# First two pairs loaded four tokens a row and turned in 112x128 blocks, second unit's values issued later

## The chip, the cores and the metric

The kernel runs on one core of one Trainium2 chip. The metric is the device time of one execution in microseconds (us); a median of several runs is given. The core has TensorE (matrix products, results in PSUM), VectorE, ScalarE, GpSimd, SyncE (SP, which here only issues transfers) and 16 DMA engines that all queues share.

## What is computed

Sigmoid attention, then a mixture of experts that sends each token to one expert:

```python
scores = q @ k^T / sqrt(64) - log(448)          # 8 batches, 12 heads, 448 tokens, 64 wide
attn   = sigmoid(scores)
x      = (attn @ v) as [8*448 tokens, 768]
logits = x @ w_gate                              # 8 experts
e      = argmax(logits); g = softmax(logits)[e]
out    = g * (relu(x @ w1[e]) @ w2[e])           # 768 -> 1024 -> 768
```

All arrays are 32-bit floats.

## The kernel before

Attention works on pairs of heads (48 pairs g, two heads of 64 on the 128 partitions) and on units of two pairs (24 units). A unit has seven steps (ST = KC = 7): a step takes every seventh token of k as 64 keys. For each step `scores(s)` multiplies k by q for both pairs (L562), ScalarE turns each pair's scores into weights by a sigmoid (`squash`, L549), and `weighted(s)` multiplies them with the values (L576) two steps behind the scores. TensorE executes in the order written; in the first steps that is scores of step s, then weighted sums of step s - 2.

k and q must stand with the head's 64 components on the partitions. From pair 2 on, `load_pair` brings them in pieces of 32 columns (128 bytes, eight DMAs a pair, q of pairs 3, 7, 9 and 11 through GpSimd's queue and the rest through SP's) and VectorE transposes 32x32 blocks (`turn`, L533). The first two pairs go another way, since nothing runs yet: `first_pair` loads each tile with one DMA, seven tokens a row (1792 bytes; k through SP, q through ScalarE's queue), and `first_turn` turns it on TensorE with 14 products by a slice of the identity (64x64, both heads beside each other; the trace records each as two), whose result VectorE (k) or ScalarE (q) copies from PSUM. Until the data are there TensorE runs 32 products of ones (`warm_up`, L540).

The values of a pair (`load_values`) come with seven tokens a row: pair 0 through ScalarE's queue, pairs 1 to 15 through GpSimd's; even pairs in one DMA, odd ones in two.

`attention` writes the order out by hand: `first_pair` for 0 and 1, the gate's weights, values of 0 and 1, warm-up, the turns, `load_pair` for 2 and 3, `load_values` for 2 and 3, then GpSimd's `blank_records` and `gate_columns`, then the steps. `READY` says behind which steps later pairs are loaded and transposed: the k of unit 2 (pairs 4, 5) is loaded from step 0 on, and so on. Tiles rotate: kn, qn, kt, qt and vn have four buffers, the weights of the sigmoid eight, the scores four PSUM banks. From step 36 on the expert layer's matmuls (L222, L241) are mixed with attention, and they fill the rest of the time.

Of the kernel before, what the change touches and what calls it, by code (L numbers as in the profile page):

```python
# [10 lines left out]
F32 = mybir.dt.float32  # L11
# [8 lines left out]
P = 128  # L20
# [5 lines left out]
def tile_sigmoid_attention_top1_moe(  # L26
# [18 lines left out]
    nc = tc.nc  # L45
    B, H, S, D = q.shape
# [3 lines left out]
    NP = H // 2  # L50
# [16 lines left out]
    small = ctx.enter_context(tc.tile_pool(name="small", bufs=1))  # L67
    ps_moe = ctx.enter_context(tc.tile_pool(name="ps_moe", bufs=2, space=bass.MemoryType.PSUM))

    ident = const.tile([P, P], F32, name="ident")  # L70
# [39 lines left out]
    def gate_columns():  # L110
        nc.gpsimd.tensor_copy(wgp[:, :, 0:E], wg)

    def blank_records():

        blank = hpool.tile([P, 1024], U32, tag=f"hl{KF - 2}", name="blank")
        blank3 = blank[:, : E * NT // P * 2].rearrange("p (r w) -> p r w", w=2)
        for w, val in enumerate((int(BIG), 0)):
            nc.gpsimd.iota(blank3[:, :, w], pattern=[[0, E * NT // P]], base=val, channel_multiplier=0)
        return lambda: nc.sync.dma_start(recs.rearrange("(p r) w -> p r w", p=P), blank3)
# [339 lines left out]
    DK = P // 2  # L459
    KC = S // DK  # L460
    ops = {}
    NG = B * NP
    OWN = [slice(h * D, (h + 1) * D) for h in range(2)]

    def quarter(g, h):

        return OWN[h if g % 2 == 0 else 1 - h]

    def load_pair(g):
        if g >= NG:  # L470
            return
        b, hp = divmod(g, NP)
        for nm, src in (("k", k), ("q", q)):
            t = apool.tile([P, S // 32, 32], F32, tag=nm + "n", bufs=4, name=f"{nm}n_{g}")
            eng = nc.gpsimd if nm == "q" and g in Q_POOL else nc.sync
            for h in range(2):
                for f in range(D // 32):
                    a = 2 * h + f
                    eng.dma_start(  # L479
                        t[32 * a : 32 * (a + 1)],  # L480
                        src[b, 2 * hp + h, :, 32 * f : 32 * (f + 1)].rearrange("(j r) s -> r j s", r=32),
                    )
            ops[g, nm + "n"] = t

    def both_heads(to, src, g, eng):
        b, hp = divmod(g, NP)
        eng.dma_start(to, src[b, 2 * hp : 2 * hp + 2].rearrange("h (p c) d -> (h p) (c d)", c=KC))

    def first_pair(g):

        t = wpool.tile([P, 1024], F32, tag="wst", bufs=RAWS_AHEAD, name=f"first_{g}")
        for n, (src, eng) in enumerate(((k, nc.sync), (q, nc.scalar))):
            both_heads(t[:, n * S : (n + 1) * S], src, g, eng)
        ops[g, "first"] = t

    def first_turn(g):

        t = ops.pop((g, "first"))
        for n, nm in enumerate("kq"):
            ps = score_tile(f"first_{g}_{nm}")  # L500
            for c in range(KC):
                for h in range(2):
                    rows, at = OWN[h], n * S + c * D
                    nc.tensor.matmul(
                        ps[rows, c * DK : (c + 1) * DK], t[rows, at : at + D], ident[rows, rows], start=True, stop=True
                    )
            to = apool.tile([P, S], F32, tag=nm + "t", bufs=4, name=f"{nm}t_{g}")
            if nm == "k":
                nc.vector.tensor_copy(to, ps[:, :S])
                ops[g, nm] = to.rearrange("d (c p) -> d c p", c=KC)  # L510
            else:
                nc.scalar.copy(to.rearrange("d (p c) -> d p c", c=KC), ps[:, :S].rearrange("d (c p) -> d p c", c=KC))
                ops[g, nm] = to

    def load_values(g):
        if g >= NG:
            return
        b, hp = divmod(g, NP)
        eng = nc.scalar if g == 0 else nc.gpsimd if g < V_POOL else nc.sync
        t = apool.tile([P, KC, D], F32, tag="vn", bufs=4, name=f"vn_{g}")  # L520
        if g % 2 == 0:
            both_heads(t.rearrange("p c d -> p (c d)"), v, g, eng)
        else:
            for h in range(2):
                eng.dma_start(t[quarter(g, h)], v[b, 2 * hp + h].rearrange("(p c) d -> p c d", c=KC))
        ops[g, "v"] = t
# [9 lines left out]
    def warm_up(n):  # L536

        ps = ps_moe.tile([P, 512], F32, tag="moe", name="ps_warm")
        for _ in range(n):
            nc.tensor.matmul(ps[:, :P], ones, ones, start=True, stop=True)  # L540

    ats, psv = {}, {}
# [9 lines left out]
    def score_tile(name):  # L552
        return ps_sc.tile([P, 512], F32, tag="sc", name=f"sc_{name}")

    def scores(s):
        u, c = divmod(s, ST)
        two = [2 * u + n for n in range(2)]
        pss = [score_tile(f"{g}_{c}") for g in two]
        for g, ps in zip(two, pss):
            for h in range(2):  # L560
                ks = ops[g, "k"][OWN[h], c]
                nc.tensor.matmul(ps[quarter(g, h), :S], ks, ops[g, "q"][OWN[h]], start=True, stop=True)  # L562
        for g, ps in zip(two, pss):
            squash(g, c, ps)
# [42 lines left out]
    def attention():  # L607

        order = ExitStack()
        order.enter_context(tc.manual_schedule())  # L610
        for g in range(2):
            first_pair(g)
        nc.gpsimd.dma_start(wg, w_gate.rearrange("(t p) e -> p t e", p=P))
        load_values(0)
        load_values(1)
        warm_up(WARM)
        first_turn(0)
        first_turn(1)
        for g in (2, 3):
            load_pair(g)  # L620
        for g in (2, 3):
            load_values(g)
        write_blank = blank_records()
        gate_columns()
        pend_gate = None
        done_av = 0

        def values(to):
            nonlocal done_av
            while done_av < min(to, N_ST):  # L630
                weighted(done_av)
                done_av += 1
                yield

        def steps(first, n, to):

            vs = values(to)
            for m in range(first, min(first + n, N_ST)):
                scores(m)
                next(vs, None)  # L640
            for _ in vs:
                pass

        for s in range(N_ST + 11):
            u, i = divmod(s, ST)
            if s in FIRST:
                wts.load(FIRST[s])
            if START - 3 < s < START:
                wts.ahead(s - START + 3, 2)
            if s < ALONE:  # L650
                steps(s, 1, s - 1)
            elif s == ALONE:
                steps(s, 1, s)
            elif i == ST - 1:
                steps(s - ST + 2, ST, s + 1)
            if s == START + 1:
                write_blank()
            elif s == START + 11:
                put_records(0)
            yield s, MIX[0]  # L660
            if s == PB + 3:
                gate_a(0)
            if i in READY and s < N_ST:
                READY[i](u)
            gb = s - PB
            if gb >= 0:
                b, r = divmod(gb, PB)
                r -= 3 if b == 0 else 2
                at = ("a" if b else None, "b", None, "c", "l", None) + (("d", "p", "e") if b else (None,) * 3 + ("d", "e"))
                what = at[r] if 0 <= r < len(at) else None  # L670
                if what == "a":
                    gate_a(b)
                elif what == "b":
                    pend_gate = gate_b(b)
                elif what == "c":
                    pend_gate = gate_c(b, *pend_gate)
                    gate_out[b] = pend_gate[0]
                elif what == "l":
                    load_regs(b)
                elif what == "d":  # L680
                    gate_d(b, *pend_gate)
                elif what == "p":
                    put_records(b)
                elif what == "e":
                    gate_e(b)
                if 3 <= r < 3 + KD // 2:
                    for t in range(2):
                        low_half(b, 2 * (r - 3) + t)
            yield s, MIX[1]
            if i in (1, 5):  # L690
                while turned:
                    token_rows(*turned.pop(0))
        order.close()
# [19 lines left out]
    for s, n in attention():  # L713
        if s >= START:
            more(n)
# [400 lines left out]
```

## Time and profile before

| | |
|---|---|
| median of 3 runs | 811.66 us (811.09 to 811.83) |
| profiled execution | 811.07 us, its span from first to last instruction 809.4 us |
| TensorE busy | 800.4 us, 99% |
| VectorE, ScalarE, GpSimd busy | 403.3, 398.1, 142.4 us |
| mean granted TensorE clock | 0.998 of full speed |
| DMA | 120.69 MB, mean 149 GB/s |

PE is TensorE and PEld its weight loads, DVE is VectorE, ACT ScalarE, POOL GpSimd; a q behind the name (SPq, POOLq) is the engine's sequencer, which issues transfers. L562 is line 562 of the kernel. Busy time of a pipelined TensorE is not TensorE at its peak. A DMA queue's share is the time that its packets took, over 16 engines' time in the window; q1 is SP's queue, q10 ScalarE's and q0 GpSimd's.

### The profile page before, as it was taken

To read this page: it belongs to the slowest core of one execution; us is meant where nothing else is said; L and a number is where in the kernel's file an instruction comes from. 1 tells how busy PE (TensorE), PEld (TensorE's weight loads), DVE (VectorE), ACT (ScalarE), POOL (GpSimd) and SP (SyncE) were. 2 spreads that over 40 slices of the span, in tenths; PEclk is the share of its full clock that TensorE was granted. 3 is DMA by queue.
4 is the path that set the end of the run, shared out by engine and by line. 5 is a ranking of instruction groups with operands and counts; after the bars stand their busy time and mean duration, and the time that the engine had idled before them with its cause. 6 is when DMAs were issued, how large, how long until landed. Compare 5 with 4: busy or idle time off the path is not lost.

```text
span 809.4 us, 15601 instructions
## 1 busy us (share of the span) xinstructions
PE 800.4 (99%) x5792; PEld 613.4 (76%) x5792; DVE 403.3 (50%) x870; ACT 398.1 (49%) x710; POOL 142.4 (18%) x212
## 2 busy tenths in 40 slices
PE   9999999999999999999999999999999999999996
PEld 5547678677687686786776876977867868999895
DVE  2466457344473265453562534833555325855561
ACT  5874745545635536446354455365463562233251
POOL 4442302110041000310022100320015001422101
PEclk9999999999999999999999999999999999999999
DMA  9999765495374663853748746548535422767761
GB/s 161 153 188 220 208 149 122 118 214 133 89 180 112 171 155 84 202 139 97 175 107 148 186 115 144 132 115 199 113 104 161 112 57 65 204 181 254 256 208 37
DMA packets 287123, 120.69 MB, mean 149 GB/s; under 512 B 200163, under 2 KB 279030, under 8 KB 287041
## 3 DMA queue, kind: packets, MB, share of 16 engines
q1 hardware_dynamic: 277792, 99.03, 51.8%
q0 software_dynamic: 8816, 19.91, 9.3%
q8 instruction: 47, 0.77, 0.4%
q10 hardware_dynamic: 432, 0.69, 0.2%
q14 instruction: 36, 0.29, 0.1%
HBM read 97.35 MB, written 23.07 MB: 149 GB/s over the span
## 4 chain that ended last, share of the span: by engine, by line
PE 95%; DMA 2%; SPq 1%; issue 1%; ACT 1%; DVE 1%; POOL 0%; POOLq 0%; DVEq 0%
PE ps L222 29%; PE ps L241 28%; PE sc L562 16%; PE av L576 15%; PE ps L926 2%; PE ps L906 2%; PE psg L275 1%; DMA kn<-in_k_dram 1%; SPq L479 1%; DMA wst<-in_moe_w_dram 0%; PE few L949 0%; ACT w1h L147 0%; PE pl L293 0%; DVE w2l L148 0%; PE pg L413 0%
## 5 line engine op out<-in xcount | busy, mean ns | idle before, releaser
L549 ACT ACTIVATE at<-sc,bias_s 128x448 f32<-128x448 f32 x336 | 196.2, 632 | 133.0 <-PE sc L562 132.0
L562 PE MATMUL sc<-qt,kt 64*64 64x448 f32 x1344 | 173.4, 544 | 0.3 <-DVE qt L533 0.3
L576 PE MATMUL av<-at,vn 64*64 64x448 f32 x1344 | 172.0, 537 | 0.0
L257 POOL DMA_DIRECT2D out_dram<-ob x96 | 61.6, 653 | 473.7 <-DVE ob L252 398.7
L241 PE MATMUL ps<-hh,w2l 128*128 128x448 f32 x384 | 142.3, 371 | 0.0
L241 PE MATMUL ps<-hh,w2h 128*128 128x448 f32 x384 | 141.8, 369 | 0.3 <-ACT w1h L147 0.3
L222 PE MATMUL ps<-xl,w1h 128*128 128x448 f32 x384 | 141.3, 368 | 0.0
L222 PE MATMUL ps<-xh,w1l 128*128 128x448 f32 x384 | 141.1, 367 | 0.0
L241 PE MATMUL ps<-hl,w2h 128*128 128x448 f32 x384 | 141.0, 367 | 0.0
L222 PE MATMUL ps<-xh,w1h 128*128 128x448 f32 x384 | 140.4, 366 | 0.0
L434 DVE STREAM_TRANSPOSE xt<-av 128x448 f32<-128x448 f32 x48 | 31.0, 646 | 211.4 <-ACT x L588 210.9
L562 PEld LDWEIGHTS sc<-qt,kt 64*64 64x64 f32 x1344 | 77.6, 189 | 61.5 <-issue 28.1
L576 PEld LDWEIGHTS av<-at,vn 64*64 64x64 f32 x1344 | 63.6, 132 | 59.8 <-issue 25.6
L227 ACT ACTIVATE hh<-ps 128x448 fp32r<-128x448 f32 x64 | 35.2, 550 | 146.1 <-PE ps L222 146.0
L147 ACT CAST w2h<-wst 128x512 fp32r<-128x512 f32 x96 | 62.0, 668 | 79.4 <-PE ps L241 67.1
L222 PEld LDWEIGHTS ps<-xl,w1h 128*128 128x128 f32 x384 | 72.1, 188 | 10.8 <-issue 5.2
L241 PEld LDWEIGHTS ps<-hh,w2h 128*128 128x128 f32 x384 | 72.2, 188 | 10.2 <-issue 4.2
L241 PEld LDWEIGHTS ps<-hh,w2l 128*128 128x128 f32 x384 | 72.2, 188 | 9.1 <-issue 3.6
L222 PEld LDWEIGHTS ps<-xh,w1l 128*128 128x128 f32 x384 | 72.1, 188 | 9.1 <-issue 3.5
L222 PEld LDWEIGHTS ps<-xh,w1h 128*128 128x128 f32 x384 | 72.1, 188 | 6.4 <-issue 0.7
L241 PEld LDWEIGHTS ps<-hl,w2h 128*128 128x128 f32 x384 | 72.2, 188 | 5.9 <-issue 0.4
L228 DVE SCALAR_TENSOR_TENSOR hl<-ps,hh 128x448 fp32r<-128x448 f32 x64 | 39.7, 621 | 71.1 <-ACT hh L227 69.4
(166 smaller groups left out, 756.3 us busy)
## 6 DMA issues: line engine op xcount, KB each, us to landing
wst<-in_moe_w_dram SPq DMA_DIRECT2D x48, 512.0 KB, 4.2
wst<-in_moe_w_dram SPq DMA_DIRECT2D x56, 384.0 KB, 4.0
x_tok<-xt SPq DMA_DIRECT2D x64, 168.0 KB, 4.5
out_dram<-ob POOLq DMA_DIRECT2D x96, 112.0 KB, 3.3
kn<-in_k_dram SPq DMA_DIRECT2D x184, 56.0 KB, 4.2
qn<-in_q_dram SPq DMA_DIRECT2D x168, 56.0 KB, 2.9
raw<-in_moe_w_dram SPq DMA_DIRECT2D x12, 512.0 KB, 4.7
kept<-in_moe_w_dram SPq DMA_DIRECT2D x12, 512.0 KB, 6.4
```

Of the source, the lines that this page charges most:

```text
L147: nc.scalar.copy(hi, st)
L222: nc.tensor.matmul(ps[:, :S], a[:, ws], b_, start=(t == 0 and n == 0), stop=(t == KD - 1 and n == 2))
L227: nc.scalar.activation(hh[:, :S], ps[:, :S], AF.Relu)
L228: nc.vector.scalar_tensor_tensor(hl[:, :S], ps[:, :S], 0.0, hh[:, :S].bitcast(F32), op0=ALU.max, op1=ALU.subtract)
L241: nc.tensor.matmul(ps[:, :S], a, b_, start=(j == 0 and n == 0), stop=(j == KF - 1 and n == 2))
L257: nc.gpsimd.dma_start(out[b * S : (b + 1) * S, cols].rearrange("(j r) f -> r j f", r=32), obv[32 * i : 32 * (i + 1)])
L434: nc.vector.transpose(xts[b, n][:, :, t, :], pv.rearrange("p (j s) -> p j s", s=32))
L549: nc.scalar.activation(at, ps[:, :S], AF.Sigmoid, bias=bias_s, scale=SCALE)
L562: nc.tensor.matmul(ps[quarter(g, h), :S], ks, ops[g, "q"][OWN[h]], start=True, stop=True)
L576: nc.tensor.matmul(psv[g][OWN[h], :S], ops[g, "v"][rows, c, :], at[rows], start=(c == 0), stop=(c == KC - 1))
L906: nc.tensor.matmul(pss[j], a[:, js], b_, start=(t == 0 and m == 0), stop=(t == KD - 1 and m == 2))
L926: nc.tensor.matmul(pss[h], a, b_[:, cs], start=(n == 0 and i == 0 and m == 0), stop=(n == 3 and i == 1 and m == 2),)
```

## The change

k and q of pairs 0 and 1 are loaded with four tokens a row on 112 partitions: one DMA a head, and the two heads side by side in each token's 128 columns, so that the pieces that land are 64 floats (256 bytes). A block of 112 tokens by 128 columns is then turned by one transposition, four for a tile, and the copy from PSUM puts the tokens in order (both copies with a strided read; k gets the view with every seventh token that all other pairs have). The values of pairs 2 and 3 are no longer issued before the steps but after the scores of the sixth step (s == 5), behind a copy of one element on GpSimd that reads that step's sigmoid weights of pair 0.

```diff
--- before.py
+++ after.py
@@ -486,31 +486,31 @@
         b, hp = divmod(g, NP)
         eng.dma_start(to, src[b, 2 * hp : 2 * hp + 2].rearrange("h (p c) d -> (h p) (c d)", c=KC))
 
+    FC = 4
+
     def first_pair(g):
 
+        b, hp = divmod(g, NP)
         t = wpool.tile([P, 1024], F32, tag="wst", bufs=RAWS_AHEAD, name=f"first_{g}")
         for n, (src, eng) in enumerate(((k, nc.sync), (q, nc.scalar))):
-            both_heads(t[:, n * S : (n + 1) * S], src, g, eng)
+            part = t[: S // FC, n * 512 : (n + 1) * 512].rearrange("p (c h d) -> p h c d", h=2, c=FC)
+            for h in range(2):
+                eng.dma_start(part[:, h], src[b, 2 * hp + h].rearrange("(p c) d -> p c d", c=FC))
         ops[g, "first"] = t
 
     def first_turn(g):
 
         t = ops.pop((g, "first"))
+        rows = S // FC
         for n, nm in enumerate("kq"):
             ps = score_tile(f"first_{g}_{nm}")
-            for c in range(KC):
-                for h in range(2):
-                    rows, at = OWN[h], n * S + c * D
-                    nc.tensor.matmul(
-                        ps[rows, c * DK : (c + 1) * DK], t[rows, at : at + D], ident[rows, rows], start=True, stop=True
-                    )
+            for c in range(FC):
+                part = t[:rows, n * 512 + c * P : n * 512 + (c + 1) * P]
+                nc.tensor.transpose(ps[:, c * rows : (c + 1) * rows], part, ident[:rows, :rows])
             to = apool.tile([P, S], F32, tag=nm + "t", bufs=4, name=f"{nm}t_{g}")
-            if nm == "k":
-                nc.vector.tensor_copy(to, ps[:, :S])
-                ops[g, nm] = to.rearrange("d (c p) -> d c p", c=KC)
-            else:
-                nc.scalar.copy(to.rearrange("d (p c) -> d p c", c=KC), ps[:, :S].rearrange("d (c p) -> d p c", c=KC))
-                ops[g, nm] = to
+            copy = nc.vector.tensor_copy if nm == "k" else nc.scalar.copy
+            copy(to.rearrange("d (p c) -> d p c", c=FC), ps[:, :S].rearrange("d (c p) -> d p c", c=FC))
+            ops[g, nm] = to.rearrange("d (p c) -> d c p", c=KC) if nm == "k" else to
 
     def load_values(g):
         if g >= NG:
@@ -618,8 +618,6 @@
         first_turn(1)
         for g in (2, 3):
             load_pair(g)
-        for g in (2, 3):
-            load_values(g)
         write_blank = blank_records()
         gate_columns()
         pend_gate = None
@@ -653,6 +651,11 @@
                 steps(s, 1, s)
             elif i == ST - 1:
                 steps(s - ST + 2, ST, s + 1)
+            if s == 5:
+                pace = small.tile([1, 1], F32, name="pace")
+                nc.gpsimd.tensor_copy(pace, ats[0, s][0:1, 0:1])
+                for g in (2, 3):
+                    load_values(g)
             if s == START + 1:
                 write_blank()
             elif s == START + 11:
```

## Rows read from the trace of the kernel before

**Rows 1.** The page: busy time of the engines; DMA queue of ScalarE (packets, MB, share).

```profile
PE 800.4 (99%) x5792; PEld 613.4 (76%) x5792; DVE 403.3 (50%) x870; ACT 398.1 (49%) x710; POOL 142.4 (18%) x212
...
q10 hardware_dynamic: 432, 0.69, 0.2%
```

**Rows 2.** The chain that ended last, 0 to 70 us: start, length, what.

```profile
7.41 2.12 SPq L479
...
11.63 5.36 DMA kn<-in_k_dram
...
18.33 0.60 PE sc L562
...
66.55 3.50 PE ps L222 x16
```

**Rows 3.** Timeline of ScalarE, 13 to 22 us: start, length, instructions, idle before.

```profile
15.16 1.35 ACT L549 ACTIVATE at<-sc,bias_s 128x448 f32<-128x448 f32 x2 [0.16 <-PE sc L562]
...
18.16 0.64 ACT L549 ACTIVATE at<-sc,bias_s 128x448 f32<-128x448 f32 x1 [0.16 <-PE sc L562]
...
20.27 1.33 ACT L549 ACTIVATE at<-sc,bias_s 128x448 f32<-128x448 f32 x2 [0.17 <-PE sc L562]
```

**Rows 4.** Timeline of VectorE, 16 to 29 us.

```profile
17.01 0.65 DVE L533 STREAM_TRANSPOSE kt<-kn 128x448 f32<-128x448 f32 x1 [1.51 <-DMA kn<-in_k_dram]
...
27.91 0.65 DVE L533 STREAM_TRANSPOSE qt<-qn 128x448 f32<-128x448 f32 x1 [2.56 <-DMA qn<-in_q_dram]
```

**Rows 5.** DMA queues, 2 to 6 us: packets, MB, share of 16 engines.

```profile
DMA packets 1674, 1.24 MB, mean 310 GB/s; under 512 B 1050, under 2 KB 1674, under 8 KB 1674
...
q10 hardware_dynamic: 427, 0.68, 49.2%
```

**Rows 6.** DMA queues, 11 to 14 us.

```profile
q0 software_dynamic: 153, 0.44, 72.1%
q1 hardware_dynamic: 1186, 0.15, 48.2%
```

**Rows 7.** DMA queues, 14 to 15 us.

```profile
q1 hardware_dynamic: 1085, 0.13, 128.0%
```

**Rows 8.** Timeline of TensorE, 3.8 to 8 us.

```profile
4.47 1.03 PE L504 MATMUL sc_first_k<-ident,first 64*64 64x64 f32 x28
...
7.78 0.55 PE L562 MATMUL sc<-qt,kt 64*64 64x448 f32 x2
```

**Rows 9.** Timeline of all engines, 743.05 to 743.7 us.

```profile
743.13 0.54 PEld L844 LDWEIGHTS px<-ident,xo 112*128 112x128 f32 x4
...
743.62 0.19 PEld L241 LDWEIGHTS ps<-hl,w2h 128*128 128x128 f32 x1
```

**Rows 10.** Timeline of VectorE, 0 to 24 us.

```profile
7.18 0.62 DVE L509 COPY kt<-sc_first_k 128x448 f32<-128x448 f32 x1 [1.01 <-PE sc_first_k L504]
```

**Rows 11.** Transfers of the first tiles: count, ns of one issue (min/median/max).

```profile
L487 SPq DMA_DIRECT2D first<-in_k_dram x2: 399/410/420, 0.9 to 1.3; - x2
```

**Rows 12.** DMA queues, 16 to 18 us.

```profile
q1 hardware_dynamic: 1016, 0.13, 41.5%
```

**Rows 13.** DMA queues, 670 to 680 us.

```profile
q1 hardware_dynamic: 1373, 0.51, 19.2%
```

**Rows 14.** Windows of two us: engines, then TensorE clock, DMA share, GB/s.

```profile
0.00:2.00 2.00, 0.70 (x7) 0.71 (x8) 0.37 (x3) 1.14 (x1) 1.31 (x12) 1.00 0.06 11
```

**Rows 15.** Timeline of GpSimd, 6 to 12 us.

```profile
7.15 0.58 POOL L487 DMA_DIRECT2D vn<-in_v_dram  x1
9.16 1.05 POOL L525 DMA_DIRECT2D vn<-in_v_dram  x2 [1.43 <-DMA wg<-in_moe_w_gate_dram]
...
10.78 0.24 POOL L111 COPY wgp<-wg 128x48 f32<-128x48 f32 x1
```

**Rows 16.** DMA issues, 7 to 7.5 us: count, KB, us to landing.

```profile
vn<-in_v_dram POOLq DMA_DIRECT2D x1, 224.0 KB, 8.3
```

**Rows 17.** DMA issues, 21.3 to 21.6 us.

```profile
vn<-in_v_dram POOLq DMA_DIRECT2D x1, 224.0 KB, 3.6
```

## The prediction

> **What bounds the kernel now.** I read the page first. TensorE is busy for 99% of the span [rows 1], so what can still move is where TensorE starts late or waits; the edit lies in the first 25 us, so only that stretch can answer. Next comes the chain that ended last, in order of time. Its front is not TensorE but the second unit's k: SP's queue, held for 2.12 us on one issue, then a kn transfer of 5.36 us, and only at 18.33 us the scores; from there to the expert matmuls at 66.55 us it is TensorE [rows 2]. The reader should see two things in it: TensorE's first scores set nothing, because the chain before 18.33 us is DMA; and what is won or lost at 18.33 us is handed down. How long TensorE stands there is read best from the sigmoids, which follow the scores at 1.50 us a step: the eighth step (first of unit 2) begins at 18.16, so the ninth should begin at 19.66 and begins at 20.27 [rows 3]. The stall is worth 0.61 us. It ends when k and q of pair 3 have been transposed, and the k transpose waited for its transfer until 17.01 [rows 4].
>
> What then bounds the transfers? The DMA windows answer: 2 to 6 us go at 310 GB/s with the big rows of the first pairs [rows 5]; from 11 to 14 us SP's queue, in 128-byte pieces, moves 1186 packets in 3 us while GpSimd's queue takes 72.1% of the engines [rows 6]; in the next microsecond, with GpSimd's done, it moves 1085 in one [rows 7]. The front is DMA-bound work of all three queues until kn of pair 3 has landed.
>
> **The change, part by part.**
>
> *Turning.* Now the four tiles are 112 recorded matmuls (28 a tile), from 4.47 until the first scores at 7.78: 3.31 us [rows 8]. Afterwards they are 16 transposes of 112x128. The trace has that very shape late in the kernel: four of them hold TensorE's weight loads from 743.13 to 743.62, 0.49 us [rows 9]. Four tiles are 1.96 us, so 1.35 us are freed, if the data are there. The copies behind them stay; VectorE's k copy, 0.62 us [rows 10], now reads with a stride, as ScalarE's q copy does already. I take it at its present price; at twice that it still lies beside the turning of q, which comes after it.
>
> *First loads.* Each tile's rows of 1792 bytes become four pieces of 256 bytes a row and head: 448 pieces a DMA, eight DMAs instead of four. Issue: two more on SP and two more on ScalarE's queue, some 0.41 us each [rows 11], so 0.82 us later for the first kn and for the first values. SP's queue is behind the DMA engines anyway, as its 2.12 us on one issue show [rows 2]. So issue costs nothing beyond the transfers; without that cover it would be 0.82 us.
> Transfer: ScalarE's queue moves 427 packets in 49.2% of 4 us on 16 engines, 73.7 ns for a 1792-byte one [rows 5]. Its three DMAs make 432 packets on the page [rows 1], 144 each: 128 rows and 16 more that close it. The four tiles are 576 packets, 576 x 73.7 / 16 = 2.65 us. Afterwards they are 8 x 464 = 3712. No row has 256 bytes. The 128-byte packets cost 13.1 ns (1016 in 41.5% of 2 us) [rows 12]; x_tok's stores, mean 371 bytes, 22.4 ns (1373 in 19.2% of 10 us) [rows 13]. In proportion between the two, 17.7 ns, which I take: 4.11 us, 1.46 more than now. Bounds: 13.1 ns gives 0.39 more, 22.4 ns 2.55 more.
> The transfers begin at about 2.0, since the engines are 6% busy before [rows 14]; so all four tiles are through at 6.1. Allowing 0.3 for landing and 0.49 for the last turn, the first scores come at 6.9, against 7.78: TensorE's front is 0.9 us earlier, not 1.35. By itself this buys nothing, since the eighth step then only stands longer.
>
> The Trainium skill speaks against this part: DMA: Bandwidth & Descriptors, section Specifications, gives 512 bytes as the least transfer for line rate, with a read-modify-write below that. Halving the 310 GB/s by it would make the first tiles some 3 us dearer by estimate, against 1.46. The row of 371 bytes (265 GB/s over 16 engines, against 389 for 1792) does not show a halving, but it is a row of stores; no run here shows loads of 256 bytes.
>
> *Values of pairs 2 and 3.* Three DMAs leave GpSimd's queue at 7.15 and 9.16 us [rows 15] and come back behind a one-element copy that waits for the sixth step's first sigmoid. They are 304 packets (144 and twice 80), 1.40 us at 73.7 ns; that is the lower bound for what their going frees. The upper: the 1186 packets of 11 to 14 us [rows 6] would take 1.1 us at 1085 a us [rows 7], so 1.9 us come free. I take 1.9, because it is SP's queue that is late and these rows show how far it is held back. The gate columns at 10.78 (0.24 us) [rows 15] and the blank records stand ahead of the copy and only come earlier.
> When are the values back? The sixth step's first sigmoid ends at 15.16 + 0.67 = 15.83 [rows 3], with the front 0.9 earlier at 14.9; the copy is at most as long as the gate columns; so the issues start at about 15.2, 15.75 and 16.3 (0.58 and 0.53 us each [rows 15]). Today pair 2's took 8.3 us to land in the crowd [rows 16]; pair 4's, issued behind 21 us, 3.6 [rows 17]. The stretch of 16 to 18 us has 41.5% busy [rows 12], so I take the second: landed at 18.8 to 19.9. They are wanted behind the tenth step's scores, at 20.27 + 1.50 = 21.8 [rows 3], 0.4 later for pair 3; a front 0.6 us earlier wants the last at 21.6. So their landing lies beside the scores of four steps with 1.7 us to spare and costs nothing; without that cover it costs what it lacks. Behind the waiting copy on GpSimd stand the values of pair 4 and q of pair 7, which wait for later work anyway.
>
> *Sum.* 1.46 - 1.90 = -0.44 by plain division; but in the crowd the queues' shares add up to 120% [rows 6], an extra packet costs less than its time, and 1.46 / 1.2 - 1.90 gives -0.68. Between the two I take -0.6 us. So the scores of the eighth step start 0.6 earlier, and that holds as far as the next tight spot: q of pair 5 is transposed from 27.91 to 28.56 [rows 4], and its scores are due at 18.33 + 7 x 1.50 = 28.83 [rows 2, 3]. That leaves 0.27 us; SP, freed earlier, must issue that q 0.33 us earlier, which I count as given. The profiled execution is 811.07 us for its span of 809.4, so 810.5 for it; it lies 0.6 below the median of the runs, 811.66. From the median: 811.0 us. Bounds: -1.9 + 0.39 = -1.5 and -1.4 + 2.55 = +1.15.
>
> **Rivals.**
> 1. *The front opens fully.* If kn lands some 1.5 us earlier, TensorE's own path decides: 0.61 of stall plus 0.9 to 1.35 of turning, 1.5 to 1.95 us, 809.7 to 810.2. For it: SP's 1085 packets in one microsecond once it is alone [rows 7]; three or four such catch up more than I counted. Against: pair 3's last kn took 5.36 us to land although it lay partly in that quick stretch [rows 2].
> 2. *Frees and extras cancel,* or pair 5's q stands at 28.56 whatever comes before it: between -0.2 and +0.7, about 811.8. For it: the values are only moved, and still lie before that q; the extra packets are new.
> 3. *Small pieces cost by the byte what the 128-byte ones do:* 26.2 ns, 6.08 us for the tiles, 3.43 more, less 1.9: +1.5, 813.2. For it: no load between 128 and 512 bytes is in this stretch. Against: the 371-byte stores [rows 13]. The Trainium skill's 512-byte rule above falls in with this case.
> 4. *Slower: the values come too late.* TensorE goes in order, so a weighted sum without its values stops the scores behind it. If pair 3's last transfer takes 8.3 us [rows 16], it lands at 24.6 for 21.6: 3.0 of stall less 0.6, +2.4, 814.1. It decides from 5.3 us after issue on. Against: the engines' 41.5% there [rows 12].
>
> **How the numbers follow.** A change of this kernel under 0.2%, 1.6 us, can hardly be told from none. Chances: my forecast (0.2 to 1.2 faster) 0.45; rival 1 0.15; rival 2 0.24; rival 3 0.09; rival 4 0.07. The likeliest gives 811.0. The range runs from rival 1's 809.7 to rival 3's 813.2; outside lie rival 4 and the far ends of 1 and 3, not over 0.15. Faster by over 0.2%: the better part of rival 1, 0.11. Slower: most of rival 4 and a third of rival 3, 0.08. Within: 0.81.
>
> **What would show it.** After the change: 16 transposes in four groups of about 0.49 us, first scores near 6.9; a 256-byte packet at 17.7 ns; near 1000 packets a us on SP's queue in 11 to 14 where there were some 400; the k transpose of pair 3 near 16.4; the ninth step's first sigmoid near 19.7; values of pairs 2 and 3 landing in under 5 us, and no wait of TensorE at 21 to 22. It would be wrong by a wait for vn there, by first tiles that land behind 6.6, or by a gain at the eighth step that q of pair 5 takes back.

## The result and the profile after

The changed kernel takes 816.07 us (median of 4 runs, 814.98 to 816.91); the kernel before, run beside it, 811.38 (810.88 to 811.83). The ratio is 1.0056, with a 95% interval of 1.0044 to 1.0068: slower by 4.7 us, outside the predicted range. The profiled executions are 815.47 and 811.07 us, 4.4 apart, so these two traces show most of the loss.

The page of the kernel after (rows as in [rows 1]): TensorE is busy 3.5 us longer with 96 instructions fewer, and ScalarE's queue 2000 packets instead of 432.

```profile
PE 803.9 (99%) x5696; PEld 614.7 (76%) x5696; DVE 403.4 (50%) x870; ACT 396.5 (49%) x710; POOL 141.8 (17%) x213
...
q10 hardware_dynamic: 2000, 0.69, 0.4%
```

TensorE's timeline from 1 to 14 us, which answers to [rows 8] and [rows 9]:

```profile
1.29 3.59 PE L540 MATMUL ps_warm<-ones 128*128 128x128 bf16 x32 [1.29 <-POOL ones L84]
5.82 0.98 PE L509 MATMUL sc_first_k<-ident,first 112*128 112x112 f32 x4 [0.94 <-DMA first<-in_k_dram]
6.60 0.95 PE L509 MATMUL sc_first_q<-ident,first 112*128 112x112 f32 x4
7.72 0.98 PE L509 MATMUL sc_first_k<-ident,first 112*128 112x112 f32 x4 [0.17 <-DMA first<-in_k_dram]
8.53 0.98 PE L509 MATMUL sc_first_q<-ident,first 112*128 112x112 f32 x4
9.44 4.35 PE L562 MATMUL sc<-qt,kt 64*64 64x448 f32 x24
```

The reader should see three things. After the warm-up TensorE waits 0.94 us for the first tile (before, it went on at 4.47). Four transposes take near 0.8 us from group to group, not 0.49. The first scores start at 9.44, not at 7.78 or at the predicted 6.9. The timeline of ScalarE shows what follows, against [rows 3]:

```profile
11.26 1.33 ACT L549 ACTIVATE at<-sc,bias_s 128x448 f32<-128x448 f32 x2 [1.18 <-PE sc L562]
...
18.07 1.16 ACT L549 ACTIVATE at<-sc,bias_s 128x448 f32<-128x448 f32 x2 [0.34 <-PE sc L562]
...
22.58 1.16 ACT L549 ACTIVATE at<-sc,bias_s 128x448 f32<-128x448 f32 x2 [0.34 <-PE sc L562]
```

The sixth step's first sigmoid is at 18.07 instead of 15.16, 2.9 later: 1.66 from the start of the scores, the rest from first scores that themselves run slowly. The ninth step's is at 22.58 instead of 20.27, only 2.3 later, because the stall of 0.61 us at the eighth step is gone. Why the stall is gone: VectorE's timeline has the k transpose of pair 3 at 14.92 where it was at 17.01 [rows 4].

```profile
14.92 0.65 DVE L533 STREAM_TRANSPOSE kt<-kn 128x448 f32<-128x448 f32 x1 [1.25 <-DMA kn<-in_k_dram]
```

The DMA window of 11 to 14 us shows SP's queue with 3061 packets instead of 1186 [rows 6], and GpSimd's with 2 instead of 153:

```profile
q1 hardware_dynamic: 3061, 0.38, 82.2%
```

So in this trace the moved values did what the prediction said (f2 below has no stall either, with the values at the old place), and the first tiles lost much more than it said. But these 2.0 to 2.3 us are only half of what the two traces differ by. The chain that ended last, after, from the first long run of expert products to the last part (L909 after is L906 before):

```profile
68.55 14.39 PE ps L222 x70
...
221.93 7.42 PE ps L241 x35
...
235.31 7.33 PE ps L241 x35
...
770.07 16.07 PE ps L909 x144
```

and the same view of before:

```profile
66.55 14.66 PE ps L222 x70
...
219.76 7.29 PE ps L241 x35
...
233.01 7.18 PE ps L241 x35
...
765.91 16.07 PE ps L906 x144
```

The run at 68.55 starts 2.0 later, the last part 4.16 later. Between them, where the change touches nothing, 2.16 us have gathered: 701.52 us instead of 699.36. The rows show how: the same 35 products take 7.42 us instead of 7.29, and 7.33 instead of 7.18 (the 70 go the other way, 14.39 for 14.66). I call the time up to the first long L222 run the *front*, and from there to the last part the *stretch*; every experiment is read by both.

### The profile page after: what moved, and what is told of

It reads as the page before. It is cut to its first block, busy times and chain, and to the rows that moved or that the text cites. A ratio compares the mean times of both kernels' runs of the same rounds, so it can differ in the third digit from the quotient of the medians.

```text
span 813.5 us, 15424 instructions
## 1 busy us (share of the span) xinstructions
PE 803.9 (99%) x5696; PEld 614.7 (76%) x5696; DVE 403.4 (50%) x870; ACT 396.5 (49%) x710; POOL 141.8 (17%) x213
## 4 chain that ended last, share of the span: by engine, by line
PE 96%; DMA 1%; DVE 1%; issue 1%; SPq 0%; ACT 0%; POOL 0%; POOLq 0%; DVEq 0%
PE ps L222 29%; PE ps L241 28%; PE sc L562 16%; PE av L576 16%; PE ps L929 2%; PE ps L909 2%; PE psg L275 1%; DMA first<-in_k_dram 1%; PE few L952 0%; DMA kn<-in_k_dram 0%; SPq L498 0%; PE pl L293 0%; DVE w2l L148 0%; PE pg L413 0%; PE px L847 0%
## 5 line engine op out<-in xcount | busy, mean ns | idle before, releaser
L562 PE MATMUL sc<-qt,kt 64*64 64x448 f32 x1344 | 169.6, 548 | 0.0
L576 PE MATMUL av<-at,vn 64*64 64x448 f32 x1344 | 166.7, 537 | 0.0
L241 PE MATMUL ps<-hh,w2l 128*128 128x448 f32 x384 | 142.8, 372 | 0.0
L241 PE MATMUL ps<-hh,w2h 128*128 128x448 f32 x384 | 142.2, 370 | 0.2 <-DVE ob L250 0.2
L241 PE MATMUL ps<-hl,w2h 128*128 128x448 f32 x384 | 141.5, 368 | 0.0
L222 PE MATMUL ps<-xl,w1h 128*128 128x448 f32 x384 | 141.5, 368 | 0.0
L222 PE MATMUL ps<-xh,w1l 128*128 128x448 f32 x384 | 141.2, 368 | 0.0
L222 PE MATMUL ps<-xh,w1h 128*128 128x448 f32 x384 | 140.5, 366 | 0.0
L562 PEld LDWEIGHTS sc<-qt,kt 64*64 64x64 f32 x1344 | 75.8, 191 | 59.6 <-issue 29.6
L576 PEld LDWEIGHTS av<-at,vn 64*64 64x64 f32 x1344 | 60.7, 132 | 60.4 <-issue 27.0
L222 PEld LDWEIGHTS ps<-xl,w1h 128*128 128x128 f32 x384 | 72.1, 188 | 11.0 <-issue 5.2
L241 PEld LDWEIGHTS ps<-hh,w2h 128*128 128x128 f32 x384 | 72.2, 188 | 10.8 <-issue 4.8
L241 PEld LDWEIGHTS ps<-hh,w2l 128*128 128x128 f32 x384 | 72.2, 188 | 9.7 <-issue 3.6
L222 PEld LDWEIGHTS ps<-xh,w1l 128*128 128x128 f32 x384 | 72.1, 188 | 9.3 <-issue 3.5
L241 PEld LDWEIGHTS ps<-hl,w2h 128*128 128x128 f32 x384 | 72.2, 188 | 6.6 <-issue 0.4
L222 PEld LDWEIGHTS ps<-xh,w1h 128*128 128x128 f32 x384 | 72.1, 188 | 6.6 <-issue 0.7
```

The source lines that it names most:

```text
L222: nc.tensor.matmul(ps[:, :S], a[:, ws], b_, start=(t == 0 and n == 0), stop=(t == KD - 1 and n == 2))
L241: nc.tensor.matmul(ps[:, :S], a, b_, start=(j == 0 and n == 0), stop=(j == KF - 1 and n == 2))
L576: nc.tensor.matmul(psv[g][OWN[h], :S], ops[g, "v"][rows, c, :], at[rows], start=(c == 0), stop=(c == KC - 1))
```

## The experiments

One table first, then each kernel. "Pieces" is the size in bytes in which the first tiles are loaded, "new tile" whether an additional small tile stands in the layout (32 bytes where nothing else is said). Front and stretch are from the chain of each profiled execution, in us.

| kernel | pieces | values moved | new tile | ratio to before [95%] | front | stretch |
|---|---|---|---|---|---|---|
| before | 1792 | no | no | 1 | 66.55 | 699.36 |
| after | 256 | yes | yes | 1.0056 [1.0044, 1.0068] | 68.55 | 701.52 |
| e1_values_moved | 1792 | yes | yes | 1.0018 [1.0008, 1.0027] | 66.48 | 701.26 |
| e2_tiles_only | 256 | no | no | 1.0043 [1.0026, 1.0060] | 68.78 | – |
| e3_warm_54 | 256 | yes | yes | 1.0038 [1.0024, 1.0052] | 68.31 | 700.54 |
| e4_1024_byte | 1024 | yes | yes | 1.0022 [1.0012, 1.0031] | 66.74 | 700.96 |
| f1_values_no_shift | 1792 | yes | no | 0.9992 [0.9983, 1.0001] | 66.00 | 699.49 |
| f2_tile_only | 1792 | no | yes | 1.0024 [1.0015, 1.0033] | 66.06 | 703.55 |
| f3_whole_no_shift | 256 | yes | no | 1.0042 [1.0027, 1.0058] | 70.16 | 699.97 |
| f4_256_byte_old_turn | 256 | no | no | 1.0035 [1.0018, 1.0052] | 69.90 | 700.33 |
| g1_1024_no_shift | 1024 | yes | no | 1.0003 [0.9993, 1.0013] | 68.31 | 698.86 |
| g2_values_64_byte_tile | 1792 | yes | yes, 64 bytes | 1.0031 [1.0018, 1.0044] | 67.02 | 702.12 |
| g3_shift_attention_only | 1792 | no | yes, in attention's pool | 1.0015 [1.0005, 1.0025] | 66.28 | 701.23 |
| g4_values_no_shift_again | 1792 | yes | no | 0.9991 [0.9981, 1.0001] | 67.04 | 699.88 |

(e2's profiled execution, 818.81 us, was the longest of its five: TensorE waits 2.9 us in it once for VectorE, at the first expert products, and its stretch is left out.)

**The second part alone.** e1 is the kernel before with the second half of the diff:

```diff
-        for g in (2, 3):
-            load_values(g)
...
+            if s == 5:
+                pace = small.tile([1, 1], F32, name="pace")
+                nc.gpsimd.tensor_copy(pace, ats[0, s][0:1, 0:1])
+                for g in (2, 3):
+                    load_values(g)
```

> The kernel before with only the second part: values of pairs 2 and 3 issued behind the sixth step's sigmoid; tiles of 1792-byte rows and the old turning stay. Theory A (the 256-byte tiles are to blame: they land late, TensorE idles after the warm-up and then runs slowly until about 13 us): the eighth step's stall of 0.61 us goes, so 0.4 to 0.8 us faster than before, 810.6 to 811.0; k of pair 3 is transposed before 15.5 us; the expert matmuls keep the pitches of before. Rival B (the later values disturb what follows): 2 us or more slower than before.

It is slower, 812.87 us for 811.51, by 1.4 us, which neither expectation had, and yet its front is no longer than before's: k of pair 3 is transposed at 13.29, and the ninth step's sigmoid comes at 20.19. The loss is in the stretch, 701.26. So something in this half harms the expert products, which begin some 50 us behind the moved issues.

**The first part alone.** e2 is the kernel after with the values issued at the old place and no `pace`:

```diff
+        for g in (2, 3):
+            load_values(g)
...
-            if s == 5:
-                pace = small.tile([1, 1], F32, name="pace")
-                ...
```

> The changed kernel with the values of pairs 2 and 3 issued where they were before; only the loading with four tokens a row and the 16 transposes are left. Theory A: as slow as the whole change or slower by up to 2 us, 816 to 818, since the values now compete again with k and q of pair 3. Rival B: near before, 811 to 812.

Measured 814.88 for 811.51: 3.4 us slower, less than theory A expected and far from rival B. The first tiles are turned from 5.98, the first scores start at 9.92: this half alone makes the loss of the front.

**A longer warm-up.** e3 is the kernel after with 54 products of ones instead of 32, so that TensorE doesn't stop ahead of the first tile.

```diff
-    WARM, V_POOL = 32, 16
+    WARM, V_POOL = 54, 16
```

> The whole change with 54 products of ones ahead of the turning in place of 32, so that TensorE has no idle time while the first tiles are on their way. Theory A, its part on TensorE's speed: the transposes take 258 ns instead of 401, the first three steps' scores 0.75 us instead of 1.5, and 1.5 to 2.5 us come back: 813.5 to 814.5. Rival C (only the tiles' arrival at 5.8 and 7.7 us counts): no change within 0.5 us, or slower by what the added products delay the first tile.

Measured 814.17 for 811.51. TensorE's timeline of e3:

```profile
6.93 0.55 PE L509 MATMUL sc_first_k<-ident,first 112*128 112x112 f32 x4
7.32 0.55 PE L509 MATMUL sc_first_q<-ident,first 112*128 112x112 f32 x4
8.93 0.57 PE L509 MATMUL sc_first_k<-ident,first 112*128 112x112 f32 x4 [1.06 <-DMA first<-in_k_dram]
9.61 0.57 PE L509 MATMUL sc_first_q<-ident,first 112*128 112x112 f32 x4
10.12 3.11 PE L562 MATMUL sc<-qt,kt 64*64 64x448 f32 x22
```

Four transposes take the predicted half microsecond again. The groups of TensorE's products in the kernel after (ns of one: least, median, most):

```profile
L540 PE MATMUL ps_warm<-ones x32: 287/314/314, 1.3 to 4.6; 128*128 128x128 bf16 x32
L509 PE MATMUL sc_first_k<-ident,first x8: 394/394/422, 5.8 to 8.3; 112*128 112x112 f32 x8
L562 PE MATMUL sc<-qt,kt x22: 536/947/1022, 9.4 to 12.9; 64*64 64x448 f32 x22
```

and in e3:

```profile
L540 PE MATMUL ps_warm<-ones x54: 219/314/314, 1.3 to 6.9; 128*128 128x128 bf16 x54
L509 PE MATMUL sc_first_k<-ident,first x8: 259/259/286, 6.9 to 9.2; 112*128 112x112 f32 x8
L562 PE MATMUL sc<-qt,kt x22: 536/536/650, 10.1 to 12.6; 64*64 64x448 f32 x22
```

TensorE begins slowly in every trace: the products of ones take 314 ns, and in some traces the last ones take 219. In e3 that comes at 6.7 us, ahead of the first tile, and the later wait of 1.06 us for k of pair 1 does not undo it. In the kernel after the 32 products end before it, none is under 287 ns, and the transposes and the first scores go on slowly until past 12 us. So TensorE did not fall back by waiting; it had not yet come up to speed. In f3 below the first transposes follow the warm-up without a wait and are slow too. Over all fourteen traces the slow pace ends between 3.8 and 6.7 us in the eleven in which TensorE doesn't pause before that, and between 12 and 14 us in the three in which it does (after, e2, f3). That the pause puts it off fits them all; no run tried it by itself.

What the slow pace costs the kernel is not shown. The two ratios differ by 0.18%, 1.5 us, and their intervals overlap; in the traces e3's ninth step has its sigmoid at 22.04 instead of 22.58, its front is only 0.24 us shorter, since the longer warm-up itself puts off the first turning, and the rest is in the stretch, which this edit doesn't touch. The wait for k of pair 1 (1.06 us) is still there: the tiles' arrival is a loss of its own.

**Larger pieces.** e4 keeps four tokens a row but stores head by head in the tile, so that a row lands in pieces of 1024 bytes; the turning is then 32 plain products of 112x64.

```diff
-            part = t[: S // FC, ...].rearrange("p (c h d) -> p h c d", h=2, c=FC)
+            part = t[: S // FC, ...].rearrange("p (h c d) -> p h c d", h=2, c=FC)
...
-                nc.tensor.transpose(ps[:, c * rows : (c + 1) * rows], part, ident[:rows, :rows])
+                for h in range(2):
+                    at = n * 512 + (h * FC + c) * D
+                    nc.tensor.matmul(
+                        ps[OWN[h], c * rows : (c + 1) * rows], t[:rows, at : at + D], ident[:rows, :rows], start=True, stop=True
+                    )
```

> The whole change, but each head's four tokens of a row stay together, so that the tiles land in pieces of 1024 bytes (112 a DMA), and are turned by 32 products of 112x64 instead of 16 transposes of 112x128. Theory A: issue falls to about 0.4 us, the first tile lands before the warm-up's end near 4.5, TensorE does not idle, and the front is that of the moved values alone: 0.4 to 1.5 us faster than before, unless the expert matmuls' pitch is worse. Rival D (four tokens a row or eight DMAs in themselves cost the time, not the pieces): stays within 1 us of the whole change, 816.

Measured 813.21 for 811.51. There are still eight DMAs, but one issue takes 0.42 to 0.44 us, the first turning starts at 4.45, and the front is 66.74: the loss of the front is gone. Its stretch is 700.96, long like e1's.

**Where the new tile is the cause.** f1 is e1 without a new tile: the pacing copy writes into `warm`, a tile that is no longer read. f2 is the opposite: nothing is moved, only the tile and its copy are added.

```diff
(f1)
-                pace = small.tile([1, 1], F32, name="pace")
-                nc.gpsimd.tensor_copy(pace, ats[0, s][0:1, 0:1])
+                nc.gpsimd.tensor_copy(warm[0:1, 0:1], ats[0, s][0:1, 0:1])
(f2, to the kernel before)
+            if s == 5:
+                pace = small.tile([1, 1], F32, name="pace")
+                nc.gpsimd.tensor_copy(pace, ats[0, s][0:1, 0:1])
```

> The moved values alone, but the one-element copy that paces them writes into an old constant tile that nothing reads any more, so that no new tile is allocated and every other tile stays at its address of before. Theory P (the new one-element tile shifts the attention tiles by 32 bytes, and with them the runs of expert matmuls fall into the slower of two pitches, 206.7 ns instead of 202.5): the 35-long runs go at 202.5 ns as before, and 1.5 to 2.2 us come back against the moved values with their tile: 810.5 to 811.3, that is 0.2 to 0.8 us faster than before. Rival Q (the later issue of the values sets the pitch): 812.5 to 813.2, pitches of 206.7 in the 35-long runs.

> The kernel before, with nothing moved, but with the one-element tile and its copy on GpSimd behind the sixth step's sigmoid. Theory P: 1.5 to 2.2 us slower than before, 813.0 to 813.7, with 206.7 ns in most of the 35-long runs. Rival Q: as before, 811.5, with 202.5 ns there.

f1 811.77, f2 814.48, for 812.37: against the kernel before both came as theory P expected. The second part without the tile loses nothing, the tile without the second part loses 0.24%. The chain of f2 has the same slow runs as the kernel after:

```profile
220.02 7.42 PE ps L241 x35
...
233.40 7.33 PE ps L241 x35
```

and the chain of f1 the fast ones of before:

```profile
219.19 7.29 PE ps L241 x35
...
232.44 7.18 PE ps L241 x35
```

What the tile does can be read from the layout of the built kernels: it takes 32 bytes of each partition, and 789 tiles that are allocated behind it lie 32 bytes further on, among them all of attention's kn, qn, kt, qt, vn and at; the tiles that the L222 and L241 products read stay where they were. (The 202.5 and 206.7 ns of the expectations are from the start of one product to the start of the next; 7.29 and 7.42 us are whole runs.)

**The whole change without the new tile.** f3 is the kernel after with f1's copy into `warm`.

> The whole change, with the pacing copy into the old constant tile. Theory P: the front stays as late as in the whole change (eighth step's first sigmoid 2 to 3 us later than before), the expert matmuls go as before: 813.3 to 814.3. Rival Q: 816.

Measured 816.14 for 812.37: 1.0042, the same as e2. That is above what theory P expected and the very number of rival Q. The trace takes the two apart: the stretch is 699.97, short, with every 35-long run at the fast pitch, as P says; the front is 70.16, longer than in the kernel after, since here k of pair 1 comes still later. By the medians taking the tile out of the whole change won only 0.14%, and the intervals of f3 and the kernel after overlap. TensorE's timeline of f3:

```profile
4.79 0.98 PE L509 MATMUL sc_first_k<-ident,first 112*128 112x112 f32 x4
5.94 0.98 PE L509 MATMUL sc_first_q<-ident,first 112*128 112x112 f32 x4 [0.17 <-DMA first<-in_q_dram]
8.48 0.98 PE L509 MATMUL sc_first_k<-ident,first 112*128 112x112 f32 x4 [1.55 <-DMA first<-in_k_dram]
9.77 0.98 PE L509 MATMUL sc_first_q<-ident,first 112*128 112x112 f32 x4 [0.31 <-DMA first<-in_q_dram]
10.68 3.27 PE L562 MATMUL sc<-qt,kt 64*64 64x448 f32 x14
```

**The pieces alone.** f4 is the kernel before with the seven tokens of a row set 72 floats apart in the tile, so that the same four DMAs carry 256-byte pieces; old turning, values at the old place.

```diff
...
-            both_heads(t[:, n * S : (n + 1) * S], src, g, eng)
+            to = t[:, n * 512 : n * 512 + 72 * KC].rearrange("p (c e) -> p c e", e=72)[:, :, :D]
+            eng.dma_start(to, src[b, 2 * hp : 2 * hp + 2].rearrange("h (p c) d -> (h p) c d", c=KC))
...
-                    rows, at = OWN[h], n * S + c * D
+                    rows, at = OWN[h], n * 512 + c * 72
```

> The kernel before in order and turning, only the first four tiles have a gap of 8 floats behind each token's 64, so that they land in pieces of 256 bytes (912 packets a DMA, four DMAs). Theory A on the front: the issues on SP and ScalarE's queue take over 1 us each instead of 0.41, the first tile lands at 5 to 6 us instead of below 4.5, TensorE idles ahead of the turning, and the whole is 1.5 to 3 us slower than before. Rival R (the number of DMAs or the four tokens a row count, not the piece): within 0.5 us of before.

Measured 814.66 for 812.37: most of the first part's loss with none of its new turning. The expected time came true, but not by the expected way: an issue takes 0.64 to 0.71 us, not over 1, the first tile is there when the warm-up ends (4.82), and TensorE is fast from there on. The first scores are only 0.7 later (8.46), but the pieces push back all that comes behind them: k of pair 3 is transposed at 19.14, the stall before the ninth step has grown from 0.61 to 2.05 us, q of pair 5 (1.2 us) and the gate (1.0 us) make TensorE wait behind it, and the front is 69.90. So the small pieces alone are enough, by a second way besides the first tiles' own lateness.

**Larger pieces, no new tile.** g1 is e4 with the copy into `warm`.

> The run with 1024-byte pieces, with the pacing copy into the old constant tile, so that no tile is shifted. If the size of the pieces and the shift are together the whole cause: no more than 0.5 us from the kernel before either way (its version with the shift was 0.22% slower, the shift costs 0.24%), and the 35-long runs at 202.5 ns. If the four tokens a row cost something of their own: 1 us or more slower than before.

Measured 812.62 for 812.29. With pieces of 1024 bytes and no shift no cost and no gain can be told from the medians. The long front of the profiled execution, 68.31, is no loss of the first tiles: the ninth step's sigmoid comes at 20.19, and then TensorE waits once, 1.5 us, for q of pair 5, the tight spot that the prediction named. The chain of g1:

```profile
21.69 1.81 SPq L479
23.54 6.16 DMA qn<-in_q_dram
...
29.83 0.66 DVE qt L536
```

Such a wait is in some executions and not in others, so a front of one trace is read with its waits.

**Which shift?** g2 makes `pace` 64 bytes ([1, 16] floats); g3 is f2 with the tile ahead of attention's own pool, so that only 572 tiles move, all of them attention's.

```diff
(g2)
+                pace = small.tile([1, 16], F32, name="pace")
+                nc.gpsimd.tensor_copy(pace[:, 0:1], ats[0, s][0:1, 0:1])
(g3)
+        pace = apool.tile([1, 1], F32, tag="pace", bufs=1, name="pace")
...
+            if s == 5:
+                nc.gpsimd.tensor_copy(pace, ats[0, s][0:1, 0:1])
```

> The moved values alone with a new tile of 64 bytes in place of 4, so that all later tiles stand 64 bytes on instead of 32. Theory P64 (only the place within 64 bytes matters): as the moved values without a new tile, 0 to 0.8 us faster than before, 202.5 ns in the 35-long runs. Rival P-any (any shift of these tiles does it): 1.3 us slower than before, 206.7 ns, as with the 4-byte tile.

> The kernel before with the one-element tile and its copy, but the tile stands ahead of the attention pool's values, k, q and weights, so that these alone are shifted by 32 bytes and the gate's small tiles stay. If TensorE's operands in attention set the pitch of the expert runs that follow: 1.5 to 2.5 us slower than before with 206.7 ns in the 35-long runs. If the gate's small tiles or the token tiles do: as before, 202.5 ns.

g2 814.29, g3 813.34, for 812.29. A shift by 64 bytes harms as much, so the theory that only the place within 64 bytes counts has fallen, though nine of the ten 35-long runs in g2 are at the fast pitch, as it expected: in g2 it is long runs of L222 that are slow (three of 98 products take 20.44 us each, for 20.05 or 20.06 before). Moving attention's tiles alone is enough for a loss, 0.15%, smaller than expected. By what the place of tiles that the expert products don't read sets their pitch stays open.

**The best version again.** g4 is f1 once more on another occasion.

> The moved values without a new tile once more, on another occasion, for the interval: if moving the values is worth something, 0.2 to 0.8 us faster than before again; if the first 0.6 was chance, within 0.2 us.

811.69 for 812.29. Both times the second part without the tile is 0.08 to 0.09% faster, 0.6 us by the medians, and both intervals just reach 1. It is the fastest of these kernels, and within what a measurement here can tell from no change.

## Why the prediction was wrong

One by one, 256-byte tiles cost 0.42% (e2, f3), the new tile 0.24% (f2) and the moved values -0.08% (f1, g4); the sum is 0.58% for a measured 0.56%. That is within the intervals, and no more: the tile is worth 0.26% between e1 and f1, 0.19% between e4 and g1, but 0.14% between the kernel after and f3, a quarter to a half of the loss. In the traces the shifted kernels have a mean stretch of 701.60 us (seven of them, 700.54 to 703.55), the others 699.65 (six, 698.86 to 700.33). Of the 35-long runs of L241 in the chains, 46 of 64 are at the slow pitch in the shifted kernels and 1 of 63 in the seven others (e2 counted here).

*Price of a packet: right.* The DMA windows of 2 to 3, 3 to 4 and 4 to 5 us of the kernel after, which answer to [rows 5]:

```profile
DMA packets 449, 0.11 MB, mean 113 GB/s; under 512 B 449, under 2 KB 449, under 8 KB 449
```
```profile
DMA packets 896, 0.22 MB, mean 221 GB/s; under 512 B 896, under 2 KB 896, under 8 KB 896
...
q10 hardware_dynamic: 510, 0.13, 56.3%
q1 hardware_dynamic: 386, 0.09, 42.2%
```
```profile
DMA packets 585, 0.15 MB, mean 146 GB/s; under 512 B 585, under 2 KB 585, under 8 KB 585
```

In the fullest of the three, 896 packets took 98.5% of 16 engines: 17.6 ns each, for the 17.7 predicted. (A straight line between the two rows that the prediction names gives 18.0, not 17.7; for all four tiles that is 0.07 us.) The Trainium skill's 512-byte rule (DMA: Bandwidth & Descriptors, Specifications) speaks of the same thing: 256 bytes in 17.6 ns are 233 GB/s over 16 engines, against the 389 of the large rows, so the row shows no halving. Pieces of 1024 bytes showed no cost (g1) and those of 256 did (f3, f4), on the two sides of that limit. But the price of a packet shows no step there: a line through the 17.6 ns for 256 bytes and the 73.7 ns for 1792 gives, by estimate, 13.0 ns for 128 bytes, where [rows 12] has 13.1. No run had a piece between 256 and 1024 bytes.

*"Issue costs nothing beyond the transfers": this step failed first.* The transfers of the first tiles in the kernel after, against [rows 11]:

```profile
L498 SPq DMA_DIRECT2D first<-in_k_dram x4: 596/622/738, 0.9 to 3.0; - x4
L498 ACTq DMA_DIRECT2D first<-in_q_dram x4: 644/658/692, 1.1 to 3.2; - x4
```

I took 0.41 us an issue from DMAs of 144 packets. With 464 packets of 256 bytes it is 0.62 to 0.66 (0.42 to 0.44 in g1, with as many DMAs of larger pieces; 0.64 to 0.71 in f4, with 912 packets of 256 bytes, so it does not grow with their number alone). SP needs 2.72 us for four, and the first kn is issued 2.1 us later, not 0.8. The cover that I named, a queue behind the DMA engines, does not exist at the start: in 2 to 5 us the engines moved 1930 packets, while 16 engines at 17.6 ns could move 2727. The chain of the kernel after says the same:

```profile
0.86 0.74 SPq L498
...
2.96 4.63 DMA first<-in_k_dram
7.72 0.98 PE sc_first_k L509 x4
```

The last k tile is issued at 2.96 and lands at 7.59, among the values and the kn that were to come behind it; I had all four tiles through at 6.1. First tiles that land behind 6.6 are one of the signs of being wrong that the prediction names.

*Turning, 1.96 us: mis-sized.* From the first transpose to the first scores it is 3.62 us (5.82 to 9.44), of which 0.17 is waiting. The 0.49 us for four transposes came from a place 740 us into the kernel [rows 9]. The prediction left out that TensorE is still slow at the start when the first tile comes late; e3 shows 0.55 us for the same four transposes once it is up to speed. This cost twice, in the turning and in the first scores, which the prediction held at their present pace. The kernel before, whose 3.31 us the prediction compared with, was up to speed when its turning began; that is chance too. In g2 the same old turning begins slowly and takes 0.7 us more for the first tile, with no late data:

```profile
4.82 1.74 PE L504 MATMUL sc_first_k<-ident,first 64*64 64x64 f32 x28
```

*A term that was missing: the new tile.* I priced the one-element copy by its time on GpSimd (0.18 us, hidden, which was right) and not its tile by its place. f2 shows that this alone costs 0.24%, and that it costs through the expert products, far behind the copy. No rival had it.

*Values: right in kind, small in size.* The freed queue brought k of pair 3 forward to 14.92, further than the predicted 16.4. The values themselves came later than I said, since the sixth step did. GpSimd's timeline, against [rows 15]:

```profile
18.77 0.18 POOL L656 COPY pace<-at 1x1 f32<-1x1 f32 x1 [10.83 <-ACT at L549]
18.89 0.59 POOL L487 DMA_DIRECT2D vn<-in_v_dram  x1
19.47 1.08 POOL L525 DMA_DIRECT2D vn<-in_v_dram  x2
```

TensorE's weight loads waited 0.2 us for them and its products not at all: rival 4 did not happen. With the old tiles (f1) the ninth step's sigmoid is at 19.70, where the prediction had it, and the median gains the predicted 0.6 us, as it does in g4, whose trace has that sigmoid at 20.74, since TensorE came up to speed later there. But no interval excludes a gain of nothing, and f2, with no values moved, has the sigmoid at 19.76: the stall of [rows 3] is not there in every execution, and a gain read from one trace was partly its chance.

*Rivals.* Rival 3 had the right part of the kernel and the right sign and a wrong mechanism: small pieces are dear through their issue and their late landing (e2, f3, f4), and at the start with a TensorE that is not yet up to speed (e2, f3), not through a packet that is dearer than the forecast said. How the loss divides between these is not shown. Rivals 1 and 2 fell with the front.

## What to carry to other kernels

Price a DMA's issue from one with pieces of the same size, and at the start of a kernel don't cover it with busy engines that are not busy yet; keep the loads that the first products wait for in large pieces. Take the durations of work at the start from the start of a kernel, not from a place where TensorE has long been running. A new tile, of four bytes too, can move the tiles behind it: write into a dead tile instead, and compare the pace of untouched loops before an edit is judged.

## What the runs showed of the hardware that was not expected

Runs of the same expert products go at one of two pitches: 35 of L241 in 7.18 to 7.29 us or in 7.32 to 7.42 (divided by 35, some 205 to 208 or 209 to 212 ns), and how many go at the slow one depends on where tiles lie that these products don't read. The place doesn't settle it alone: the kernel after and e3 place every tile alike, and nine of nine are slow in the one, six of nine in the other. The seven shifted kernels all have a longer stretch than the six others; the mechanism was not found, and the nearest two (700.33 and 700.54) are close, so a single trace would not have shown it.

In the front of the kernel after, matmuls take 947 instead of 536 ns and transposes 394 instead of 259, while the granted clock of that window reads 1.00 like everywhere, the upper of its two levels (2.4 GHz). The warm-up products speak otherwise: in the kernel before they follow each other every 107 ns at first and every 55 to 56 ns from 4.04 us on, a factor of two as between 1.2 and 2.4 GHz, and that column reads 1.00 in both. So durations show this state, that column doesn't. The window of 10 to 12 us of the kernel after (engines, clock, DMA share, GB/s):

```profile
10.00:12.00 2.00, 2.00 (x14) 0.91 (x14) 0.00 (x0) 0.76 (x3) 0.00 (x0) 1.00 1.19 171
```
